# Neighbouring weight columns in a turned projection, and a re-ordered turnover between two MoE layers

## The chip, the cores and the metric

The kernel runs on one core of one Trainium2 chip. The metric is the device time of one execution in microseconds; lower is better. The kernel before was timed in three runs, and one more execution was profiled.

## The reference

Three layers follow each other. Attention over 2 x 8 heads of 768 tokens by 64, in which a query sees only keys with the same six sign bits of a projection. A dense mixture of four experts over the 1536 tokens of width 512: `out += p[:, e] * (relu(x @ w1[e]) @ w2[e])`, hidden width 1024. And a second mixture of eight experts, in which a noisy gate chooses two per token:

```python
noisy_logits = x @ w_gate + log1p(exp(x @ w_noise)) * noise
top2 = argpartition(-noisy_logits, 2)[:, :2]          # weights: softmax of the two
for e in range(8):
    for k in range(2):
        mask = top2[:, k] == e
        out[mask] += top2_w[mask, k, None] * (relu(x[mask] @ w1[e]) @ w2[e])
```

All is float32. The kernel writes each factor of a large matmul as a rounded high part and a rest (`fp32r`, names ending in h and l) and sums three products, so each product of the reference is three matmuls.

## The kernel before, in words

**The second MoE.** The 1536 tokens are routed into a table in DRAM (`tv`), 432 slots (`CAP`) per expert; slots without a token point at padding rows. Expert e needs its rows of `x2d` gathered (GpSimd's indirect DMAs), turned so that the model dimension lies across partitions (`rows`: gh, gl), and its weights loaded and split: a part of 512 KB is loaded into one of four `stage` buffers (`stage_part`, L168, issued by SP), copied to the high part (L175 or L177) and subtracted (L179). For each expert TensorE runs a hidden layer of four parts (`hidden_part`, L212 to L214, 24 matmuls each; relu on ScalarE L217, remainder on VectorE L219) and a projection.

Experts 1 to 6 use the turned projection (`project_turned`, L867 to L869): for each d of four, 24 matmuls with w2 columns as stationary operand and the 432 slots as 432 moving columns. Chunk d takes the columns 4m + d of w2 (`by_chunk`), that is, columns that lie four apart. ScalarE copies the result from PSUM (L871), VectorE transposes it in 32x32 blocks into `yt` (L872), SP stores it to `yd` in DRAM (L876) and loads it back as `ya`, one row per slot (L880). During the next expert `send` multiplies each quarter of `ya` in place by the gate's weight (L691), and GpSimd scatters it into the output with an accumulating indirect DMA (L693). In the same loop VectorE and ScalarE turn the next expert's rows (`turn_blocks`, L855 to L859) and split the next w1 (`load_w1_part`). Experts 0 and 7 use a straight projection (`project`, L233 to L235, 512 moving columns) and multiply and scatter directly (`put`).

**The turnover.** The last expert of the first MoE works in four chunks of tokens. When the last chunk is projected (L716), its three tiles of 128 tokens are stored, turned (`turn_tile`, L563), rated (`tile_logits`, L572), their experts chosen (`choose`, L585 to L601, short operations on 8 columns on VectorE), placed (`place`, L609 to L646: a matmul for the running counts, then two scatters per tile into the table). Expert 0 of the second MoE is split: its first 216 slots (`EARLY`) come from earlier chunks, and its hidden layer (216 moving columns) starts before the last tiles are placed; the three `place` calls stand between its parts. The other 216 slots are fetched after the last scatter (`fetch`: a load of the list `lt` L658, then two gathers L663) and turned (L672 to L676) after three quarters of the early part's second projection. `list_rows` loads the lists of the other experts (L822, L826).

In the last part of the first MoE only TensorE's order is written by hand and a scheduler orders the other engines; from `wt1 = wt1_next` on, the order on every engine and queue is that of the program. w2 of expert 0 is loaded and split inside the first hand-written stretch (`load_w2(w2b, 0, nc.gpsimd)`: both steps on GpSimd). The w1 parts of expert 1 are loaded by SP in order behind `list_rows`. `fetch_blocks` for expert 2 (16 gathers) stands in expert 0's late hidden layer.

## Time and profile before

| | us |
|---|---|
| median of three runs (lowest, highest) | 1178.85 (1178.27, 1178.87) |
| profiled execution, own time | 1177.99 |
| its span | 1176.2 |
| TensorE busy with matmuls | 1145.1 |
| VectorE, GpSimd, ScalarE busy | 607.3, 476.1, 399.8 |
| mean granted TensorE clock, share of full | 0.986 |

The profile is one execution; times in its trace are microseconds from the start of the span. A row of the timeline gives the start, the duration, the engine (PE is TensorE, DVE VectorE, ACT ScalarE, POOL GpSimd, SP SyncE; a q behind the name is its instruction queue, which issues DMAs), the line, the operation, output and inputs, and in brackets a wait ahead of it and who ended it. PEld are weight loads. Matmul durations overlap, so the distance from start to start tells their pace.

### The profile page before, as it was taken

How to read it: one execution, taken by the hardware profiler on the slowest of the kernel's cores; microseconds unless marked ns; L12 is line 12 of the kernel's file. 1: busy time of each engine (PE TensorE's matmuls, PEld its weight loads, DVE VectorE, ACT ScalarE, POOL GpSimd, SP SyncE). 2: the span in 40 equal slices, each digit the busy share in tenths (PEclk: the TensorE clock that was granted, in tenths of full speed). 3: DMA queues.
4: the chain of work that ended last, by engine and by line, in shares of the span. 5: the costliest groups of instructions: out<-in, count | busy, mean ns of one | idle time of the engine just before them, and what ended most of it. 6: DMA issues, size and time to landing. Idle time of an engine off the chain costs nothing. (4 is left out here: it accounts for less than half of the span.)

```text
span 1176.2 us, 16395 instructions
## 1 busy us (share of the span) xinstructions
PE 1145.1 (97%) x6278; PEld 1053.8 (90%) x6279; DVE 607.3 (52%) x1239; ACT 399.8 (34%) x759; POOL 476.1 (40%) x498
## 2 busy tenths in 40 slices
PE   7999999999999999999999999999799999999995
PEld 5999999999899998988999988898689999999993
DVE  7999999985213411242213323356246566656650
ACT  5999998961111100001111111121033333433330
POOL 7888888852001100030001102136377165585233
PEclk9999999999999999999999999997899999999998
DMA  4222222372002200031001200031455556766754
GB/s 137 69 64 66 68 69 68 87 235 72 1 1 65 79 1 1 1 101 43 1 1 54 90 28 28 1 101 41 98 144 165 179 146 195 216 155 200 189 128 58
DMA packets 78539, 101.23 MB, mean 86 GB/s; under 512 B 12944, under 2 KB 54032, under 8 KB 77808
## 3 DMA queue, kind: packets, MB, share of 16 engines
q1 hardware_dynamic: 66888, 84.84, 24.0%
q0 software_dynamic: 9728, 15.18, 6.9%
q8 instruction: 51, 0.84, 0.3%
q10 hardware_dynamic: 1840, 0.11, 0.1%
q14 instruction: 32, 0.26, 0.1%
HBM read 73.30 MB, written 20.90 MB: 80 GB/s over the span
## 5 line engine op out<-in xcount | busy, mean ns | idle before, releaser
L217 ACT ACTIVATE hh<-big 128x768 fp32r<-128x768 f32 (+2 forms) x100 | 81.2, 812 | 495.6 <-PE big L214 467.9
L219 DVE SCALAR_TENSOR_TENSOR hl<-big,hh 128x768 fp32r<-128x768 f32 (+2 forms) x100 | 95.7, 957 | 243.5 <-ACT hh L217 243.2
L233 PE MATMUL sm<-w2h,hh 128*128 128x512 f32 (+1 forms) x448 | 177.5, 397 | 0.0
L234 PE MATMUL sm<-w2l,hh 128*128 128x512 f32 (+1 forms) x448 | 176.3, 394 | 0.0
L212 PE MATMUL big<-xth,w1h 128*128 128x384 f32 x512 | 173.6, 339 | 0.0
L214 PE MATMUL big<-xth,w1l 128*128 128x384 f32 x512 | 172.4, 337 | 0.0
L213 PE MATMUL big<-xtl,w1h 128*128 128x384 f32 x512 | 172.2, 336 | 0.0
L235 PE MATMUL sm<-w2h,hl 128*128 128x512 f32 (+1 forms) x448 | 171.5, 395 | 0.0
L177 POOL TENSOR_SCALAR w1h<-stage 128x1024 fp32r<-128x1024 f32 x18 | 18.8, 1048 | 341.5 <-PE big L213 338.1
L849 POOL DMA_INDIRECT xb<-x2d,at x96 | 112.4, 1171 | 29.4 <-issue 28.7
L251 POOL TENSOR_SCALAR ex<-ex,rec 128x768 f32<-128x768 f32 x96 | 94.0, 979 | 32.6 <-DVE rec L378 21.1
L395 DVE TENSOR_TENSOR el<-sm,eh 128x384 fp32r<-128x384 f32 x192 | 97.5, 547 | 11.8 <-ACT eh L394 10.2
L235 PEld LDWEIGHTS sm<-w2h,hl 128*128 128x128 f32 (+1 forms) x448 | 83.4, 186 | 20.6
L234 PEld LDWEIGHTS sm<-w2l,hh 128*128 128x128 f32 (+1 forms) x448 | 83.7, 187 | 19.5
L212 PE MATMUL big<-gh,w1h 128*128 128x432 f32 (+1 forms) x288 | 101.1, 351 | 0.0
L213 PE MATMUL big<-gl,w1h 128*128 128x432 f32 (+1 forms) x288 | 100.7, 350 | 0.3 <-DVE gl L676 0.3
L214 PE MATMUL big<-gh,w1l 128*128 128x432 f32 (+1 forms) x288 | 100.3, 348 | 0.0
L233 PEld LDWEIGHTS sm<-w2h,hh 128*128 128x128 f32 (+1 forms) x448 | 83.4, 186 | 18.7
L213 PEld LDWEIGHTS big<-xtl,w1h 128*128 128x128 f32 x512 | 96.4, 188 | 1.0
L212 PEld LDWEIGHTS big<-xth,w1h 128*128 128x128 f32 x512 | 96.4, 188 | 0.9
L214 PEld LDWEIGHTS big<-xth,w1l 128*128 128x128 f32 x512 | 96.3, 188 | 0.0
L356 PE MATMUL big<-k,q 128*128 128x512 f32 (+1 forms) x384 | 89.8, 356 | 2.4 <-POOL k L342 2.4
(198 smaller groups left out, 2279.4 us busy)
## 6 DMA issues: line engine op xcount, KB each, us to landing
stage<-in_moe_w_dram SPq DMA_DIRECT2D x96, 512.0 KB
yd<-yt SPq DMA_DIRECT2D x24, 216.0 KB
ya<-yd SPq DMA_DIRECT2D x6, 864.0 KB
out_dram<-zero SPq DMA_DIRECT2D x1, 4096.0 KB
qr<-in_q_dram SPq DMA_DIRECT2D x16, 192.0 KB
kr<-in_k_dram SPq DMA_DIRECT2D x16, 192.0 KB
vr<-in_v_dram SPq DMA_DIRECT2D x16, 192.0 KB
q<-q SPq DMA_DIRECT2D x15, 192.0 KB
```

Of the source, the lines that this page charges most:

```text
L212: nc.tensor.matmul(o, wh[:, d, fs], xh[:, d, cols], start=(d == 0), stop=False)
L213: nc.tensor.matmul(o, wh[:, d, fs], xl[:, d, cols], start=False, stop=False)
L214: nc.tensor.matmul(o, wl[:, d, fs], xh[:, d, cols], start=False, stop=(d == ND - 1))
L217: nc.scalar.activation(hh, pv, AF.Relu)
L219: nc.vector.scalar_tensor_tensor(hl, pv, 0.0, v32(hh), op0=ALU.max, op1=ALU.subtract)
L233: nc.tensor.matmul(o, hh[:, ff, cols], wh[:, ff], start=(f == 0), stop=False)
L234: nc.tensor.matmul(o, hh[:, ff, cols], wl[:, ff], start=False, stop=False)
L235: nc.tensor.matmul(o, hl[:, ff, cols], wh[:, ff], start=False, stop=(f == NF - 1))
L251: engine.tensor_scalar(o, i, scale, bias, op0=ALU.mult, op1=ALU.add)
L356: nc.tensor.matmul(ps[:, n0:n1], w_[:, qs], x_[:, n0:n1], start=st, stop=not st)
L395: nc.vector.tensor_sub(el[:, cs, js], ptv, v32(eh)[:, cs, js])
L849: nc.gpsimd.indirect_dma_start(out=xb[:, b], out_offset=None, in_=x2d.rearrange("t (g x) -> (t g) x", g=4), in_offset=bass.IndirectOffsetO ...
```

## The change

The turned projection takes 128 neighbouring columns of w2 per chunk instead of columns four apart; so `yt` and `yd` hold the columns in another order (g k c instead of k g c, runs of 32), and `send` puts them right while it multiplies, into a new tile with the tag `xg` instead of in place. At the turnover, the last of the four early hidden parts moves behind the hand-over to the full hand-written order; w2 of expert 0 is only loaded in the first stretch, and split by ScalarE and VectorE, two parts ahead of that hidden part and two behind it. `list_rows` is issued by ScalarE instead of SP, and stands behind the turning of the late rows; behind it ScalarE issues the four loads of expert 1's w1, which the splits in expert 0's late projection then use. Of the 16 gathers of `fetch_blocks` for expert 2, four stand behind each late projection of expert 0 and four each in the second and fourth hidden part of expert 1.

```diff
@@ -163,9 +163,9 @@
                             pad_b.rearrange("p j c -> p (j c)").unsqueeze(1).to_broadcast([P, E2, 2 * OVER_J]))
-    def stage_part(src, shape):
+    def stage_part(src, shape, queue=nc.sync):
         st = stage.tile(shape, F32, tag="stage", name="stage")
-        nc.sync.dma_start(st, src)
+        queue.dma_start(st, src)
         return st
     def load_part(wp, bufs, src, shape, tag, engine=nc.gpsimd, rest=nc.vector, staged=None):
@@ -687,8 +687,8 @@
     sent = {}
-    def scatter(y, ps, lt, s, e):
-        nc.vector.tensor_scalar_mul(y, ps, lt[:, s, 1:2].bitcast(F32))
+    def scatter(y, ps, lt, s, e, view=None):
+        nc.vector.tensor_scalar_mul(y if view is None else view, ps, lt[:, s, 1:2].bitcast(F32))
         nc.gpsimd.memset(apart, 0.0)
         ins = nc.gpsimd.indirect_dma_start(out=out, out_offset=bass.IndirectOffsetOnAxis(ap=lt[:, s, 0:1], axis=0),
                                            in_=y, in_offset=None, compute_op=ALU.add)
@@ -777,17 +777,17 @@
         store(t3 + 2, 1)
         chosen = [choose(tile_logits(turned[0]), t3, 1)]
         turned.append(turn_tile(t3 + 1))
-        rows = [ap.tile([P, ND, EARLY], F32R, tag=t, name=t) for t in ("gh", "gl")]
+        first_rows = [ap.tile([P, ND, EARLY], F32R, tag=t, name=t) for t in ("gh", "gl")]
         for s in range(early):
-            turn_rows(rows, s, xgs)
+            turn_rows(first_rows, s, xgs)
         turned.append(turn_tile(t3 + 2))
         chosen.append(choose(tile_logits(turned[1]), t3 + 1, 1))
         parts = []
-        for g in range(NP):
+        for g in range(NP - 1):
             between = (lambda: place(*chosen[2], t3 + 2, 1, base_late)) if g == 2 else None
-            parts.append(hidden_part(g, wt1_next, *rows, EARLY, slice(0, EARLY), between))
+            parts.append(hidden_part(g, wt1_next, *first_rows, EARLY, slice(0, EARLY), between))
             if g == 0:
-                wt2 = load_w2(w2b, 0, nc.gpsimd)
+                staged = [stage_part(w2_part(w2b, 0, r), [P, 2, DM]) for r in range(NP)]
                 chosen.append(choose(tile_logits(turned[2]), t3 + 2, 1))
                 place(*chosen[0], t3, 1, base_late)
             if g == 1:
@@ -819,11 +819,11 @@
     nc.gpsimd.memset(at, 0)
     def list_rows():
-        nc.sync.dma_start(lts[:, 1:].rearrange("p e s c -> p e (s c)"),
+        nc.scalar.dma_start(lts[:, 1:].rearrange("p e s c -> p e (s c)"),
                           tv[1:, 0:CAP].rearrange("e (p s) c -> p e (s c)", p=SLOT_P))
         src = tv[2:, 0:CAP].rearrange("e (b r s) c -> b r e (s c)", b=4, r=BLOCK)
         for b in range(4):
-            nc.sync.dma_start(li[:, 2:, b].rearrange("r e s c -> r e (s c)"), src[b])
+            nc.scalar.dma_start(li[:, 2:, b].rearrange("r e s c -> r e (s c)"), src[b])
     def list_pieces():
         for g in range(4):
@@ -863,13 +863,13 @@
         for f in range(NF):
             g, ff = divmod(f, 2)
             hh, hl = parts[g]
-            wh, wl = (by_chunk(w[:, ff], d) for w in wt[g])
+            wh, wl = (w[:, ff, d * P:(d + 1) * P] for w in wt[g])
             nc.tensor.matmul(ps[:, :CAP], wh, hh[:, ff], start=(f == 0), stop=False)
             nc.tensor.matmul(ps[:, :CAP], wh, hl[:, ff], start=False, stop=False)
             nc.tensor.matmul(ps[:, :CAP], wl, hh[:, ff], start=False, stop=(f == NF - 1))
         yp = padded[d % 2]
         nc.scalar.copy(yp[:, :, :, :BLOCK], ps[:, :CAP].rearrange("p (s b r) -> p s b r", s=SLOT_S, b=4))
-        nc.vector.transpose(yt.rearrange("p s b (c k) -> p k (s b) c", k=ND)[:, d], yp.rearrange("p s b r -> p (s b) r"))
+        nc.vector.transpose(yt.rearrange("p s b (k c) -> p k (s b) c", k=ND)[:, d], yp.rearrange("p s b r -> p (s b) r"))
     def store_turned(yt):
         for g in range(4):
@@ -880,13 +880,18 @@
         nc.sync.dma_start(ya, yd.rearrange("(p s) d -> p s d", s=SLOT_S))
         return ya
     def send(s, ya, e):
-        scatter(ya[:, s], ya[:, s], lts[:, e], s, e)
+        y = mp.tile([SLOT_P, DM], F32, tag="xg", name="xg", bufs=SLOT_S)
+        scatter(y, ya[:, s].rearrange("p (g k c) -> p k g c", g=4, k=ND), lts[:, e], s, e,
+                y.rearrange("p (k g c) -> p k g c", g=4, k=ND))
     with tc.manual_schedule():
         wt1 = wt1_next
+        wt2 = [load_w2_part(w2b, 0, r, engine=nc.scalar, staged=staged[r]) for r in (0, 1)]
+        parts.append(hidden_part(NP - 1, wt1, *first_rows, EARLY, slice(0, EARLY)))
+        wt2 += [load_w2_part(w2b, 0, r, engine=nc.scalar, staged=staged[r]) for r in (2, 3)]
         lt_late, xgs = fetch(mp, SLOT_S, 0, EARLY, early)
-        list_rows()
         rows = new_rows(early)
         give(ap, "xg", early, parts, wt2, lt, 0, 0)
         ps = small()
@@ -894,6 +899,8 @@
         project(ps[:SLOT_P], parts, wt2, mine, 0, 6)
         for s in range(early):
             turn_rows(rows, s, xgs)
+        list_rows()
+        staged = [stage_part(w1_part(w1b, 1, r), [P, ND, FC], nc.scalar) for r in range(NP)]
         project(ps[:SLOT_P], parts, wt2, mine, 6, NF)
         put(ap, "xg", early, ps, lt, 1, 0)
         late = []
@@ -918,8 +925,8 @@
                 if g == 1 and e == 0:
                     list_pieces()
                     xbs[2] = blocks()
-                if g >= 2 and e == 0:
-                    fetch_blocks(2, xbs[2], (g - 2) * 8, (g - 1) * 8)
+                if g in (1, 3) and e == 1:
+                    fetch_blocks(2, xbs[2], 6 + 2 * g, 10 + 2 * g)
             if e + 1 < E2:
                 wt1 = []
                 rows = new_rows(SLOT_S)
@@ -941,8 +948,9 @@
                 for s in range(n):
                     for r in range(s * SLOT_S // n, (s + 1) * SLOT_S // n):
                         turn_rows(rows, r, xgs)
-                        wt1.append(load_w1_part(w1b, e + 1, r, nc.scalar))
+                        wt1.append(load_w1_part(w1b, e + 1, r, nc.scalar, staged[r]))
                     give(mp, "y", 2, parts, wt2, lt_late, s, 0)
+                    fetch_blocks(2, xbs[2], 4 * s, 4 * s + 4)
             else:
                 for s in range(n):
                     give(mp, "xg", SLOT_S, parts, wt2, lts[:, e], s, e)
```

## Rows read from the trace of the kernel before

**Rows 1.** The page, part 1: busy time, share of the span and instructions.
```profile
PE 1145.1 (97%) x6278; PEld 1053.8 (90%) x6279; DVE 607.3 (52%) x1239; ACT 399.8 (34%) x759; POOL 476.1 (40%) x498
```

**Rows 2.** Timeline of TensorE: first matmul of expert 1's hidden layer, projection, and of expert 2.
```profile
872.72 0.36 PE L212 MATMUL big<-gh,w1h 128*128 128x432 f32 x1
...
891.70 0.40 PE L867 MATMUL sm<-hh,w2h 128*128 128x432 f32 x1
...
914.14 0.36 PE L212 MATMUL big<-gh,w1h 128*128 128x432 f32 x1
```

**Rows 3.** Groups by line and shape, weight loads: count, then busy us, mean ns, idle before.
```profile
L867 PEld LDWEIGHTS sm<-hh,w2h 128*128 128x128 f32 x192 | 63.2, 329 | 0.1
...
L212 PEld LDWEIGHTS big<-gh,w1h 128*128 128x128 f32 x288 | 56.8, 197 | 2.4
```

**Rows 4.** Timeline of TensorE at the turnover.
```profile
808.78 0.55 PE L213 MATMUL big<-gl,w1h 128*128 128x216 f32 x1 [0.30 <-DVE gl L676]
...
817.46 0.19 PE L619 MATMUL sm<-both,tri 128*128 128x8 bf16 x1 [1.88 <-DVE both L609]
...
825.48 0.35 PE L212 MATMUL big<-gh,w1h 128*128 128x216 f32 x1
...
828.23 0.40 PE L233 MATMUL sm<-w2h,hh 128*108 128x512 f32 x1
...
844.02 0.97 PE L672 MATMUL sm<-ident,xg 108*128 108x108 f32 x4 [5.97 <-issue]
...
867.07 0.46 PE L233 MATMUL sm<-w2h,hh 128*108 128x512 f32 x1
```

**Rows 5.** Short windows: length, busy PE, PEld, DVE, ACT, POOL, granted clock, DMA share, GB/s.
```profile
808.00:810.00 2.00, 1.70 (x9) 1.48 (x8) 2.00 (x7) 0.58 (x2) 2.00 (x3) 0.62 0.03 8
...
822.00:824.00 2.00, 2.00 (x21) 1.96 (x20) 1.28 (x12) 0.53 (x1) 0.90 (x1) 0.96 0.07 5
...
842.00:844.00 2.00, 0.00 (x0) 0.01 (x1) 0.00 (x0) 0.00 (x0) 0.00 (x0) 0.66 1.10 241
...
848.00:850.00 2.00, 2.00 (x12) 1.77 (x11) 0.75 (x1) 0.00 (x0) 0.11 (x1) 0.64 0.00 0
```

**Rows 6.** Timelines of GpSimd and VectorE at the turnover.
```profile
804.54 2.37 POOL L179 TENSOR_TENSOR w2l<-stage,w2h 128x1024 fp32r<-128x1024 f32 x1
...
804.82 2.11 DVE L585 SCALAR_TENSOR_TENSOR na<-lg 128x8 f32<-128x8 f32 x1
...
819.57 0.16 DVE L585 SCALAR_TENSOR_TENSOR na<-lg 128x8 f32<-128x8 f32 x1
```

**Rows 7.** SP's list and weight loads; landing times of L663, L838 (gathers), L646 (scatters).
```profile
831.40 1.63 SPq L826 DMA_DIRECT2D li<-table  x4
...
833.13 3.15 SPq L168 DMA_DIRECT2D stage<-in_moe_w_dram  x4
...
DMA to landing us min/median/max: 3.7/5.8/8.0
...
DMA to landing us min/median/max: 3.8/3.9/4.0
...
DMA to landing us min/median/max: 2.1/2.5/5.2
```

**Rows 8.** Single lines: splits of w2 and the multiplies, duration in ns min/median/max.
```profile
L175 ACT CAST w2h<-stage x28: 1039/1044/1054, 878.4 to 1137.2; 128x1024 fp32r<-128x1024 f32 x28
...
L179 DVE TENSOR_TENSOR w2l<-stage,w2h x44: 1206/1215/2062, 280.2 to 1138.2; 128x1024 fp32r<-128x1024 f32 x44
...
L691 DVE TENSOR_SCALAR ya<-ya,lts x24: 397/469/534, 946.1 to 1143.6; 108x512 f32<-108x512 f32 x24
...
L691 DVE TENSOR_SCALAR y<-sm,lt x2: 749/750/751, 866.4 to 872.9; 108x512 f32<-108x512 f32 x2
```

**Rows 9.** Timeline in expert 5: the last row tile for expert 6, and its first use.
```profile
1073.60 0.61 DVE L859 TENSOR_TENSOR gl<-tb,gh 128x432 fp32r<-128x432 f32 x1 [0.62 <-ACT gh L858]
...
1079.88 0.36 PE L212 MATMUL big<-gh,w1h 128*128 128x432 f32 x1
```

## The prediction

> **What bounds the kernel now.** The page's first part comes first: TensorE is busy for 1145.1 of 1176.2 us, no other engine for more than 52% [rows 1]. So a change is worth what it takes from TensorE's time, in two ways: matmuls that follow each other faster, or gaps and slow-clock stretches that go. The profiled execution took 1177.99 us, 1.8 us more than its span; the median of the runs is 1178.85, 0.07% above it. I sum against 1177.99; about 0.2% (2.4 us) is what a measurement of this kernel can tell from no change.
>
> The timeline of TensorE's queue comes second, at the borders of one expert of the second MoE. Expert 1's 96 hidden matmuls run from 872.72 to 891.70, its 96 turned-projection matmuls from 891.70 to 914.14 [rows 2]: 197.7 ns against 233.8 ns from start to start, both with 432 moving columns, neither with a gap. The same two durations, 18.99 and 22.44 us, return in the six experts 1 to 6. What differs is the weight load: 197 ns when its 128 columns are neighbours, 329 ns when they lie four floats apart [rows 3]. A hidden part with 216 moving columns shows how fast neighbouring columns can be loaded: 24 loads and matmuls from 825.48 to 828.23, 115 ns each [rows 4]. Twice that is 229 ns, close to the 233.8. I read the turned projection as paced by its weight loads, and the hidden layer with 432 columns as paced by the moving operand.
>
> The same timeline and short windows of the granted clock show the turnover, 808 to 850 us. TensorE waits 0.30, 1.88 and 5.97 us [rows 4]. A window that averages 0.62 between two levels, full (2.4 GHz) and half (1.2 GHz), puts the first fall at 808.5; it rises at 822.2, falls again at 842.6 and rises at 849.4 [rows 5]. The low stretches hold 13.7 and 6.8 us; less the waits in them, TensorE works 11.5 and 5.4 us at half rate, and half of that, 5.75 and 2.7, is lost. Waits and half rate together: 8.15 + 8.45 = 16.6 us. That is all the turnover can give.
>
> **The change, part by part.**
>
> Neighbouring weight columns. Each of 6 x 96 = 576 matmuls then loads a contiguous slice and streams the same 432 columns as the hidden layer, so I take the hidden layer's pace: 22.44 - 18.99 = 3.45 us an expert, **20.7 us** in six. All of it is on TensorE's path. Bounds: 0 if the loads were not the pace; not more than 20.7, as the hidden layer at 432 columns goes no faster in any of seven experts.
> The Trainium skill ("TensorE: Matmul & The Clock Gate", "Part 2: What happens when you issue a matmul") says that weights come through a read port of their own and are pulled ahead of running matmuls; with its "Back-to-back issue gap", N/2.4 + 2.5 ns, 432 columns would take an estimated 182.5 ns whatever the layout, and this part would bring nothing. [rows 2] speak against it: the two stages differ by 36 ns at equal columns. By that rule the sum would be the second rival's.
>
> The permuted output. The projection now leaves VectorE's transposes writing runs of 32 floats instead of single floats 16 bytes apart, at the same count; I take no gain. `send` multiplies out of `ya` through a permuted view into a fresh tile instead of in place. Before, it took 469 ns in the middle; a multiply of 108x512 out of PSUM took 0.75 us [rows 8]. I take 0.75, so +0.28 us on 24 sends, between 0 and, say, a doubling to 0.94. It is covered: in expert 5 the last row tile for the next expert (L859) ends at 1074.21, and TensorE needs it at 1079.88 [rows 9], 5.7 us later. The shorter stage takes 3.45 of these, one longer send ahead of it 0.3; 1.9 us stay, and some of VectorE's present waits are for evacuations that come earlier now. Cost 0. The fresh `ya` reader has a good side: the reload of `ya` no longer waits for the output scatters, so SP is free sooner for the weight loads behind it. Cost and gain 0 on TensorE. In expert 7 the four sends hold all four `xg` buffers until their scatters land, so the first two multiplies of the last expert may wait some microseconds; four PSUM buffers take the four results, and the last multiply does not wait. Cost 0.
>
> w2's split off GpSimd. While GpSimd subtracts (2.37 us), VectorE's 8-element operation takes 2.11 us; the same one takes 0.16 us when GpSimd rests [rows 6]. Five of them are stretched between 804 and 817, and the router's chain behind them is what TensorE waits 1.88 us for (`both`, L609), and probably the 0.30. These waits go. Instead ScalarE copies four parts (1.04 us each) and VectorE subtracts (1.22 each) [rows 8] around the last hidden part. Let t be the end of the third hidden part. Behind relu and remainder of that part the four subtractions end at about t+3.0, 4.2, 6.0 and 7.2, with the fourth part's relu (t+3.5) and remainder (t+4.8) between. TensorE ends the fourth part at t+2.75 and needs a new w2 part every 1.4 us from there, the small half 0.2 us later: t+3.0, 4.4, 5.8, 7.2. I charge **0.3 us**, 0 to 1.5.
>
> The first clock fall. What stands ahead of 808.5 is unchanged, so I let it fall again. The second time the rate rose 5.4 us after work resumed [rows 5]; without the 1.88 us wait I give the first stretch about 4 us of work at half rate, lost **2.0 us** (0 if it does not fall, 5.75 if it stays low as long).
>
> The late gather. Here 5.97 us go. Just ahead of the two gathers SP issues the lists' loads, four of them in 1.63 us, and from 833.13 four 512 KB weight loads in 3.15 us [rows 7]. Gathers took 3.7 to 8.0 us to land here, and 3.8 to 4.0 where no weights were loading [rows 7]. Now these loads and the five list loads stand behind the gathered rows' casts on ScalarE's own queue. The six table scatters follow each other on GpSimd; one lands 2.5 us after its issue in the middle [rows 7], and with the router unhindered the last does so at about t+5. ScalarE reaches the load of the rows' list (`lt`) behind its four copies at t+5.5; with 2.4 us for that load, as small as a scatter, the gathers issue at t+7.9 and t+9.2 and land 3.7 later, t+11.6 and t+12.9. TensorE, through 2.75, 5.6 (867.07 to 872.72, [rows 2, 4]) and three quarters of that again, wants them at t+12.6 and t+13.1. I charge **0.3 us**, 0 to 3; the second clock fall has no cause left.
>
> What the moved loads now meet. ScalarE issues 5 small and 4 large loads, 2.0 + 3.2 us at SP's durations [rows 7], ahead of the relu of expert 0's first late part. TensorE can run two parts (5.5 us) and the rest of a projection (1.4) until it wants that PSUM buffer back; ScalarE's cast, issues and relu and VectorE's remainder end at about 7.6. I charge **0.7**, 0 to 2. The gathers for expert 1 now share the engines with the 2 MB: issued at about 4 us after the casts and landing in up to 8, the first two come 12 to 13.5 us after, and TensorE wants them 12.4 after: **0.5**, 0 to 2; with landings of 4 us the term would be 0.
> The Trainium skill ("DMA: Bandwidth & Descriptors", "Issuing engines are not separate DMA queues") says that the queues of all issuing engines run on the same 16 DMA engines: by that rule the move to ScalarE's queue buys no bandwidth, only another order, and the collision is real (the 0.5); were ScalarE's queue a path of its own, the sum would be 0.5 lower. The loaded landing of 8.0 us, gathers of one queue beside loads of another, agrees with the rule.
> `fetch_blocks` for expert 2 is moved past two scatters; GpSimd has no other work then, and even with the landing at expert 1's projection VectorE starts on them 2 us in. Cost 0.
>
> The sum: turnover 16.6 - (0.3 + 2.0 + 0.3 + 0.7 + 0.5) = 12.8; I take **12.4**, the rest for the small waits I don't see. 1177.99 - 20.7 - 12.4 = 1144.9, forecast **1145 us**. Turnover by the bounds: 16.6 down to 2.35 if every charge came at its upper end; I hold 8 for the likely floor, as the charges are for independent waits. Likeliest case: 1140.7 to 1149.3.
>
> **The rivals.**
> First, the turnover's wait only moves: ScalarE's nine issues and four copies, or the collision, eat most of the 16.6, leaving 2.35 (every charge at its upper end) to 4. For it: ScalarE is one in-order queue and relus stand behind. Against: each is under 1 us by the sums. Time: 1177.99 - 20.7 - 3 = 1154.
> Second, the weight loads are not the pace (other order of operands, PSUM writes), and joining brings nothing: 1177.99 - 12.4 = 1165.6. Against: [rows 3] and the 115 ns of [rows 4].
> Third, slower: VectorE becomes the pace of the six turned stages, because the permuted multiply is far dearer than I take it. From a send of 2.4 us on (0.47 + 1.9) the next expert's rows come late by the rest; to end slower than before it must also cost back 33.1/6 = 5.5 us a stage, that is some 8 us a send. At 10 us: 7.6 late in six stages, less 33.1 gained, 1190. Against: same bytes, runs of 32 floats.
>
> **How the numbers follow.** Forecast 0.82, first rival 0.08, second 0.06, third 0.02; 0.02 for a mixture near no change. The range: from 1140.7 to 1152, which takes in what lies between forecast and first rival; outside stay about 2 in 10. Faster by over 0.2%: 0.82 + 0.08 + 0.06 = 0.96, within 0.02, slower 0.02.
>
> **What would show it.** Six projection stages of 19.0 us with weight loads of about 197 ns; the first wait for `both` gone and VectorE's router operations at 0.15 us throughout; the third hidden part ending about 6 us earlier; no wait over 1 us for the late rows and full clock from 815 on; sends near 0.75 us with no wait of the hidden layer for `gh` or `gl`. The prediction is wrong if the projection keeps 22.4 us, if TensorE waits for ScalarE's relu or w2 between the late gather and expert 1, or if the clock stays at half through the early half of expert 0.

## The result and the profile after

The changed kernel takes 1148.53 us (median of 4 runs, 1146.85 to 1150.78), the kernel before 1178.56 us in the same comparison: a ratio of 0.975 with an interval of 0.973 to 0.977, or 30.0 us less. The forecast was 1145.0 us, the range 1140.7 to 1152.0. The profiled execution is the longest of the four, 1150.78 us with a span of 1149.0, 27.2 us under the profiled execution of before.

The page's first part after, which answers to [rows 1]:

```profile
PE 1120.7 (98%) x6278; PEld 1025.1 (89%) x6279; DVE 595.8 (52%) x1243; ACT 403.1 (35%) x763; POOL 458.7 (40%) x490
```

TensorE's busy time falls by 24.4 us at the same count of instructions: most of the gain is matmuls that take less time, not gaps that went.

TensorE's timeline at the borders of expert 1 (against [rows 2]), then the groups of the turned projection (against [rows 3]; columns: count, busy us, mean ns, idle before):

```profile
867.38 0.36 PE L212 MATMUL big<-gh,w1h 128*128 128x432 f32 x1
...
886.35 0.36 PE L867 MATMUL sm<-hh,w2h 128*128 128x432 f32 x1
...
905.07 0.36 PE L212 MATMUL big<-gh,w1h 128*128 128x432 f32 x1
```

```profile
L867 PEld LDWEIGHTS sm<-hh,w2h 128*128 128x128 f32 x192 | 36.1, 188 | 1.4
...
L867 PE MATMUL sm<-hh,w2h 128*128 128x432 f32 x192 | 68.5, 357 | 0.0
```

The hidden layer keeps its 18.97 us. The turned projection goes from 22.44 to 18.72 us, and its weight load from 329 to 188 ns. The other five turned experts have the same two durations, so the columns give 6 x 3.72 = 22.3 us in this trace.

The turnover in TensorE's timeline (against [rows 4]), with the waits in brackets, and the granted clock in short windows (against [rows 5]; columns as there):

```profile
807.74 0.70 PE L672 MATMUL sm<-ident,xg 108*128 108x108 f32 x4 [0.81 <-DMA xg<-x2d,lt]
809.53 0.70 PE L672 MATMUL sm<-ident,xg 108*128 108x108 f32 x4 [1.09 <-DMA xg<-x2d,lt]
...
836.95 0.70 PE L672 MATMUL sm<-ident,xg 108*128 108x108 f32 x4 [0.33 <-issue]
838.11 0.73 PE L672 MATMUL sm<-ident,xg 108*128 108x108 f32 x4 [0.46 <-DMA xg<-x2d,lt]
...
851.58 0.73 PE L672 MATMUL sm<-ident,xg 108*128 108x108 f32 x4 [0.62 <-DMA xg<-x2d,lts]
853.21 0.73 PE L672 MATMUL sm<-ident,xg 108*128 108x108 f32 x4 [0.91 <-DMA xg<-x2d,lts]
```

```profile
808.00:810.00 2.00, 0.91 (x8) 0.77 (x8) 0.61 (x1) 0.52 (x1) 0.00 (x0) 1.00 0.47 179
810.00:812.00 2.00, 2.00 (x12) 2.00 (x12) 0.68 (x2) 1.21 (x3) 0.00 (x0) 0.54 0.00 0
816.00:818.00 2.00, 2.00 (x16) 2.00 (x15) 0.00 (x0) 0.44 (x1) 0.00 (x0) 0.75 0.00 0
854.00:856.00 2.00, 2.00 (x7) 1.47 (x6) 2.00 (x3) 1.44 (x2) 0.00 (x0) 0.63 0.49 160
```

The waits of 1.88 and 5.97 us are gone. In their place stand three pairs: for the early rows (1.90 us together), the late rows (0.79) and expert 1's rows (1.53). The clock falls after the first pair, to half from 810.2 to 817.0, and after the third, from about 854.5 to 858.0.

An account by stretch makes the profiles comparable. I take the stretch from the first matmul with `both` (L619, near 785 us) to expert 1's first hidden matmul, sum TensorE's waits in it, and sum (1 - granted clock) x length over 1 us windows: that is what half rate costs TensorE if it works all the time. A wait at half rate is counted in both, so the remainder is too small where waits were long.

```
                stretch   waits   half rate   remainder
before           88.76     8.97     10.24       69.55
after            81.61     4.22      5.13       72.26
```

The stretch gives 7.15 us, not the 12.4 of the forecast. The work ahead of it starts 1.8 us later in this execution (785.77 against 783.96; the order there is the same). 22.3 + 7.15 - 1.8 = 27.7 us, and the two profiled executions differ by 27.2: the difference is accounted for.

One more group changed size. VectorE's transposes of the projection's results (L872) and the sends (L691, against the 469 ns of [rows 8]), duration in ns min/median/max; first the transposes in the kernel before, then both after:

```profile
L872 DVE STREAM_TRANSPOSE yt<-padded x24: 1110/1121/1128, 898.3 to 1122.1; 128x512 f32<-128x512 f32 x24
```

```profile
L872 DVE STREAM_TRANSPOSE yt<-padded x24: 704/706/712, 894.6 to 1094.3; 128x512 f32<-128x512 f32 x24
...
L691 DVE TENSOR_SCALAR xg<-ya,lts x24: 444/478/572, 935.4 to 1115.8; 108x512 f32<-108x512 f32 x24
```

The transposes fall by 415 ns, which the forecast had at nothing; the sends stay where they were.

Finally GpSimd's two gathers of the early rows and, just ahead of them, VectorE's two subtractions for parts 0 and 1 of the new `w2`:

```profile
802.81 2.38 DVE L179 TENSOR_TENSOR w2l<-stage,w2h 128x1024 fp32r<-128x1024 f32 x2 [1.31 <-ACT w2h L175]
...
803.01 1.91 POOL L663 DMA_INDIRECT xg<-x2d,lt  x1 [5.54 <-issue]
805.23 1.00 POOL L663 DMA_INDIRECT xg<-x2d,lt  x1 [0.30 <-issue]
```

The forecast had these subtractions around the last hidden part, at 820 to 830 us. They stand behind `wt1 = wt1_next`, from where the order is said to be that of the program, but that did not keep them behind the router's operations, which the program has ahead of them: the scheduler put them at 802 us, where the wait ahead of them, 1.31 us, is for ScalarE's copy. The first gather's issue beside them takes 1.91 us where the second takes 1.00. This is the line that the experiments go after.

### The profile page after: what moved, and what is told of

It is laid out like the page before. It is cut to its first block, busy times and chain, and to the rows that moved or that the text cites. A ratio compares the mean times of both kernels' runs of the same rounds, so it can differ in the third digit from the quotient of the medians.

```text
span 1149.0 us, 16369 instructions
## 1 busy us (share of the span) xinstructions
PE 1120.7 (98%) x6278; PEld 1025.1 (89%) x6279; DVE 595.8 (52%) x1243; ACT 403.1 (35%) x763; POOL 458.7 (40%) x490
## 5 line engine op out<-in xcount | busy, mean ns | idle before, releaser
L219 DVE SCALAR_TENSOR_TENSOR hl<-big,hh 128x768 fp32r<-128x768 f32 (+2 forms) x100 | 95.8, 958 | 246.8 <-ACT hh L217 246.3
L849 POOL DMA_INDIRECT xb<-x2d,at x96 | 104.7, 1091 | 29.3 <-issue 29.3
L235 PEld LDWEIGHTS sm<-w2h,hl 128*128 128x128 f32 (+1 forms) x448 | 83.5, 186 | 20.7
```

The costliest lines, as they stand in the source:

```text
L219: nc.vector.scalar_tensor_tensor(hl, pv, 0.0, v32(hh), op0=ALU.max, op1=ALU.subtract)
L235: nc.tensor.matmul(o, hl[:, ff, cols], wh[:, ff], start=False, stop=(f == NF - 1))
L849: nc.gpsimd.indirect_dma_start(out=xb[:, b], out_offset=None, in_=x2d.rearrange("t (g x) -> (t g) x", g=4), in_offset=bass.IndirectOffsetO ...
```

## The experiments

The runs came in three groups, each on a chip of its own; times are compared within a group, beside the kernel before on that chip (group 1: 1179.55 us; group 2: 1195.09; group 3: 1197.42).

**Group 1: the two halves of the change, apart and together.** First the columns alone: the kernel before with the joined columns, the permuted transposes and the new `send`.

```diff
-            wh, wl = (by_chunk(w[:, ff], d) for w in wt[g])
+            wh, wl = (w[:, ff, d * P:(d + 1) * P] for w in wt[g])
```

> The kernel before with the neighbouring columns alone (the permuted transposes and the permuted send go with them, the turnover is the old one). Theory: the turned projection was paced by its weight loads, and the gain of the columns doesn't depend on the turnover: six projection stages of 18.7 us instead of 22.44, 22.3 us off the kernel before, about 1156.3. Also by it: the second gather for expert 0's early rows is issued about 1.0 us behind the first, since VectorE then runs no split of w2, and TensorE waits about 0.6 us for it. Rival: part of the 22 us comes only with the other turnover (weight loads from DRAM that come late in the shorter stages): then TensorE waits for w1 or w2 and the gain is under 20 us, above 1159.

Measured: 1156.58 us (1155.61 to 1157.27), 23.0 us less, ratio 0.981 (0.979 to 0.982). Loads and transposes are those of after (188 and 704 ns), and the turnover keeps the two old waits, the first of them longer than the 1.88 us of before:

```profile
818.85 0.19 PE L619 MATMUL sm<-both,tri 128*128 128x8 bf16 x1 [5.02 <-DVE both L609]
...
846.31 1.69 PE L672 MATMUL sm<-ident,xg 108*128 108x108 f32 x8 [6.03 <-issue]
```

It follows that the columns carry three quarters of the gain by themselves, with nothing given back.

Then the turnover alone: the kernel after with the old columns, transposes and in-place `send`.

```diff
-            wh, wl = (w[:, ff, d * P:(d + 1) * P] for w in wt[g])
+            wh, wl = (by_chunk(w[:, ff], d) for w in wt[g])
```

> The changed kernel with the old columns (four apart), the old transposes and the in-place send; the turnover is the new one. Theory: the turnover gives what is left of the whole, 30.0 - 22.3 = 7.7 us, about 1170.9, instead of the 12.4 that were forecast, because TensorE still waits for the early gather (about 1.9 us), for expert 1's first two gathers (about 1.5 us) and loses a second stretch at the half clock behind the latter. Rival: the turnover gives the forecast 12.4 (1166.2) by itself and loses in the whole through something that the columns bring.

Measured: 1167.45 us (1163.94 to 1173.99), 12.1 us less, ratio 0.991 (0.987 to 0.994). Here the turnover gives what the forecast said, though the runs reach over 10 us, and its stretch is 76.32 us. In this profile the gather's issue starts 0.09 us ahead of the subtraction, not behind it:

```profile
802.30 1.02 POOL L663 DMA_INDIRECT xg<-x2d,lt  x1 [5.01 <-issue]
803.62 1.00 POOL L663 DMA_INDIRECT xg<-x2d,lt  x1 [0.30 <-issue]
...
802.39 1.23 DVE L179 TENSOR_TENSOR w2l<-stage,w2h 128x1024 fp32r<-128x1024 f32 x1 [1.77 <-ACT w2h L175]
```

Both issues take 1.0 us, TensorE does not wait for the early rows, and the first clock fall is missing. The wait for expert 1's rows is there (1.53 and 0.33 us), with a fall of the clock behind it.

The kernel after again, beside these two:

> The changed kernel again, to have it beside the others on one chip, and a second trace. Theory: the 4 us between its runs (1146.85 to 1150.78) are the first 30 us and the clock: where the mean granted clock is higher, the run is shorter. About 1148.5; in this trace the two waits for expert 1's gathers and for the early gather stand again. Rival: the waits in the turnover were chance of one execution and are absent here.

Measured: 1149.93 us (1142.89 to 1151.91), ratio 0.974 (0.971 to 0.976). The profile shows the slow issue (1.91 us), early waits of 0.58 and 1.02 us, and half clock from 807.9 to 825. The two halves sum to 35.1 us by their medians and the whole gives 29.6; by the ratios they sum to 2.9% and the whole gives 2.7%, which their intervals don't tell apart. That the halves take something from each other is not shown. The runs go largely with the granted clock: 1151.91 us at a mean of 0.984, 1142.89 at 0.994.

Expert 1's gathers earlier: `list_rows` right behind `fetch`, `fetch_rows(1)` ahead of the second early scatter.

```diff
         lt_late, xgs = fetch(mp, SLOT_S, 0, EARLY, early)
+        list_rows()
...
-        list_rows()
+        xgs = fetch_rows(1)
...
-                if g == 0 and e == 0:
-                    xgs = fetch_rows(1)
```

> The changed kernel, with the lists of the other experts loaded right behind the late rows' list, and expert 1's four gathers issued ahead of the second early scatter, so that they are issued before most of w1's 2 MB are in flight; w1's loads stay. Theory: the collision of these gathers with the 2 MB makes TensorE wait 0.6 and 0.9 us and drops its clock for about 3.4 us, so that taking the gathers out of the collision gives back 1.5 + 1.7 = 3.2 us: about 1145.3. Rival: TensorE waits there for something else (ScalarE, busy with issuing nine DMAs, casts late): then the waits stay, and the time is within 1 us of the changed kernel.

Measured: 1146.94 us (1144.90 to 1150.52), ratio 0.974 (0.972 to 0.975). The gathers are issued from 835.0 instead of 846.2 us, and the wait for expert 1's rows (0.31 and 0.66 us in the run of the kernel after beside it, without a fall of the clock of its own) is gone. They land as slowly as before the edit (median 8.8 us, against 8.0). The median is 3.0 us lower than that of the kernel after, but the two sets of runs overlap: the time is not shown to be better.

**Group 2: the race and the collision.** The kernel after was not run on this chip, so no time here says what an edit is worth beside it; the traces say what each edit did. First the subtractions put behind the early rows' second `gl` on VectorE, by an order on that engine alone (`turned_last` is that instruction):

```diff
+        with tc.issue_after(turned_last):
-        wt2 = [load_w2_part(w2b, 0, r, engine=nc.scalar, staged=staged[r]) for r in (0, 1)]
+            wt2 = [load_w2_part(w2b, 0, r, engine=nc.scalar, staged=staged[r]) for r in (0, 1)]
```

> The kernel after, with VectorE's subtractions for the first two w2 parts of the second MoE queued behind its second `gl` of the early rows (same engine, order alone; in the kernel after they stand ahead of the third accumulation of tile 15's group, at 802 us). Theory (a race of 0.2 us at 802 us): in three profiles where such a subtraction had begun before GpSimd issued the first early gather, that issue took 1.91 us, and in the one profile where it had not, 1.02 us; the slow issue puts the second gather 0.9 us later, TensorE waits 1.6 to 1.8 us for the early rows and its granted clock falls. So here: both gather issues 1.0 us, early waits together under 0.6 us, no stretch at the lower clock between 803 and 825 us, 76 to 78 us from the first matmul of `both` to expert 1's hidden part (82.7 in the second profile of the kernel after), time 1143.5 to 1146. Rival (the slow issue comes of something else that stands there, such as the accumulations' traffic or the loads): issue 1.9 us as before, time 1148 to 1151. Third case: the subtractions now delay VectorE's chain of the router by their 2.5 us and the late rows come later: wait for them 2 us or more, time about 1147.

Measured: 1171.03 us (1161.52 to 1172.56), ratio 0.978 (0.974 to 0.981). The trace does most of what the theory says: both issues are fast, there is no half clock anywhere in the stretch, and the stretch is 76.77 us; the early wait is 0.80 us, where under 0.6 was expected.

```profile
802.82 1.02 POOL L663 DMA_INDIRECT xg<-x2d,lt  x1 [5.42 <-issue]
804.15 1.00 POOL L663 DMA_INDIRECT xg<-x2d,lt  x1 [0.30 <-issue]
...
809.95 1.22 DVE L179 TENSOR_TENSOR w2l<-stage,w2h 128x1024 fp32r<-128x1024 f32 x1
811.16 1.22 DVE L179 TENSOR_TENSOR w2l<-stage,w2h 128x1024 fp32r<-128x1024 f32 x1
```

The window from 803 to 860 us (columns as in [rows 5]) has the full clock throughout:

```profile
803.00:860.00 57.00, 52.89 (x360) 46.01 (x359) 28.50 (x110) 17.08 (x34) 20.78 (x24) 1.00 0.39 102
```

The third case came too, in small: the subtractions now stand ahead of the router chain, and TensorE waits 0.98 us for `both`. The absolute time can't be set beside group 1. On this chip TensorE waits another 18.2 us in expert 1's projection, which no profile of group 1 has (last section).

Both edits together:

> The kernel after with two edits at once: the subtractions behind `gl` (as in the run before this) and the lists with expert 1's gathers issued ahead of the second early scatter. If the two causes are separate (the slow first gather; expert 1's rows landing after they are wanted), the gains add: no early wait over 0.3 us, none for expert 1's rows, one short stretch at the lower clock at most, 75 to 76.5 us from `both` to expert 1's hidden part, time 1142 to 1144.5. If the clock's fall is one event that either edit prevents or that comes anyway, it gives what the better of the two gives alone: 1145 to 1147.

Measured: 1167.06 us (1165.88 to 1170.89), ratio 0.976 (0.975 to 0.978), stretch 77.24 us. Expert 1's rows are not waited for, the issues are fast, but the clock falls once, behind the 0.98 us wait for `both`. By this one profile it is the second outcome, that the gains don't add; how far a single profile can be trusted here shows in group 3.

The collision tried from the other side: the four loads of expert 1's `w1` behind the gathers.

```diff
-        staged = [stage_part(w1_part(w1b, 1, r), [P, ND, FC], nc.scalar) for r in range(NP)]
...
+                if g == 1 and e == 0:
+                    staged = [stage_part(w1_part(w1b, 1, r), [P, ND, FC], nc.scalar) for r in range(NP)]
```

> The kernel after with the four loads of expert 1's w1 (2 MB, on ScalarE's queue) issued behind the second relu of the late hidden part instead of ahead of the first: some 5 us later, behind the issues of expert 1's four gathers. Theory (these loads are what the gathers collide with): the gathers land 3.8 to 5 us after their issue instead of 8, TensorE waits under 0.3 us for expert 1's rows (1.0 to 1.5 in the kernel after). Against that, ScalarE's copies of the w1 parts stand between its copies of the rows, and the first part now lands 5 us later, near 853 us, so that a wait for rows may come from there: up to 2 us. Time 1147 to 1150. Rival (the gathers are slow for another reason: their lists' loads, or 108 rows at a time on this queue): landing 7 to 8 us as before and the waits stay; time 1150 to 1153, since the loads too are late.

Measured: 1170.13 us (1167.46 to 1176.64), ratio 0.980 (0.976 to 0.983), stretch 76.78 us. TensorE takes expert 1's rows with no wait:

```profile
850.27 1.14 PE L672 MATMUL sm<-ident,xg 108*128 108x108 f32 x8
```

The early issue is slow here (1.97 us, the subtraction having begun 0.15 us before it), with early waits of 0.38 and 1.09 us. The view of expert 1's gathers has no landing times here, and the vanished wait alone would leave a landing of up to 7.6 us open (issue at 842.68, first use at 850.27). The DMA packets in the trace settle it. Behind the first issue GpSimd's queue moves 192 packets of 4 KB, which hold most of the rows. A quarter of them has ended 3.72 us after that issue and half after 4.62 us, as for the same gathers in the kernel before (3.73 and 4.64), where after has 6.51 and 8.27. The last quarter ends at 11.11 us, as late as in after (11.25), now that the loads run beside it. The collision is shown, for the gathers that TensorE waits for.

**What a weight load pays for distance.** Columns two apart, in the kernel after:

```diff
-            wh, wl = (w[:, ff, d * P:(d + 1) * P] for w in wt[g])
+            wh, wl = (w[:, ff, (d // 2) * 256 + d % 2:(d // 2) * 256 + d % 2 + 255:2] for w in wt[g])
```

> The kernel after with the turned projection's weight columns two apart (0, 2, 4, ... 254 and so on) instead of neighbouring; the output's columns of the six turned experts then come out in another order, with the same work. Before, columns four apart had weight loads of 329 ns and a stage of 22.44 us; neighbouring ones have 188 ns and 18.72 us. If the cost of a load grows evenly with the distance, loads take about 235 ns and the stage, which at 18.72 us is held by the moving columns, stays within 18.7 to 19.5 us: time 1147 to 1155. If any distance other than one costs the whole price: loads 329 ns, stage 22.4 us, time about 1172. If two apart is as good as one: 188 ns, 18.7 us, time as the kernel after.

And eight apart:

```diff
-            wh, wl = (w[:, ff, d * P:(d + 1) * P] for w in wt[g])
+            wh, wl = (w.rearrange("p c d -> p (c d)")[:, 4 * ff + d:4 * ff + d + 1017:8] for w in wt[g])
```

> The kernel after with the turned projection's weight columns eight apart, taken across both 512-column halves of a w2 part; the six turned experts then multiply other columns than the reference's, with the same amount of work. Loads took 188 ns with neighbouring columns, 194 ns with columns two apart and 329 ns with columns four apart. If from there on every column costs a fetch of its own: about 330 ns, stage 22.4 us, 22 us more than the kernel after. If the cost goes on growing with the distance: about 600 ns, and a stage of 40 us or more, over 120 us more.

Measured in the traces: the load (ns, min/median/max) and one projection stage (window, its length, busy times) of the kernel with two apart, then of that with eight apart:

```profile
L867 PEld LDWEIGHTS sm<-hh,w2h x192: 193/194/330, 892.9 to 1119.0; 128*128 128x128 f32 x192
...
949.81:968.62 18.81, 18.81 (x97) 18.68 (x96) 13.73 (x17) 7.21 (x11) 5.73 (x4) 1.00 0.47 132
```

```profile
L867 PEld LDWEIGHTS sm<-hh,w2h x192: 313/344/351, 883.1 to 1140.7; 128*128 128x128 f32 x192
...
948.10:971.62 23.52, 23.52 (x97) 23.51 (x97) 13.94 (x17) 7.50 (x11) 8.11 (x7) 1.00 0.36 104
```

So loads of 188, 194, 329 and 344 ns and stages of 18.72, 18.81, 22.44 and 23.52 us, for columns 1, 2, 4 and 8 floats apart. The price comes whole between two and four apart and hardly grows behind; neither an even growth nor "any distance costs" holds. The times are of one run each. Eight apart takes 1198.75 us, 28.2 more than the kernel after on the same chip (1170.51, group 3), where the six stages give 6 x 4.80 = 28.8. Two apart takes 1176.93 us on the chip of group 2, where the kernel after was not run.

**Group 3: the two edits made better, beside the kernel after.** The subtractions behind the first late tile's `both` (`placed` collects these instructions), and expert 1's loads of `w1` behind the gathers, as above:

```diff
+        with tc.issue_after(placed[-3]):
```

> The kernel after with two edits: VectorE's first two w2 subtractions of the second MoE queued behind the first late tile's `both` (in the run e5_subs_later, behind `gl`, they stood in front of that tile's router chain and TensorE waited 0.98 us for it), and expert 1's w1 loads issued behind the late hidden part's second relu, as in e7_loads_later. If the two causes that were found are separate (the early gather's issue slowed by a VectorE subtraction that began before it; expert 1's gathers landing beside 2 MB of loads): both early issues 1.0 us, no wait for `both` over 0.5 us, none for expert 1's rows over 0.3 us, no lower clock between 803 and 860 us, 74 to 75.5 us from `both` to expert 1's hidden part (82.7 in the kernel after's second profile, 76.8 in each of the two edits alone): 5 to 8 us under the kernel after on the same chip. If the clock falls all the same, 2 to 4 us under it.

> The kernel after once more, on the same chip as the runs beside it, as what they are compared with. By the race: where its profile shows a w2 subtraction begun before the first early gather's issue, that issue takes 1.9 us; where not, 1.0 us, and then the early wait and the fall of the clock at 808 to 825 us are missing too. Ratio to the kernel before 0.972 to 0.977.

> The kernel of e5_subs_later once more, beside the kernel after. Its stretch from `both` to expert 1's hidden part was 76.8 us with no lower clock, against 81.4 and 82.7 us in the two profiles of the kernel after: 4 to 6 us under the kernel after if that was typical, under 2 us if the kernel after often runs without the slow issue.

Measured: the combined kernel 1173.01 us (1164.78 to 1173.77), ratio 0.979 (0.977 to 0.982); the kernel after 1170.51 (1166.71 to 1176.79), 0.980 (0.977 to 0.983); the subtractions behind `gl` 1168.19 (1163.29 to 1173.84), 0.976 (0.973 to 0.979). None is told from another. The combined kernel's trace has no half clock and no wait for `both` or expert 1's rows, but it has a new one, 1.77 us ahead of the late rows' transposes, and its stretch is 76.60 us, not 74 to 75.5. The subtractions behind `gl`, the same kernel as in group 2, now take 82.44 us: waits of 0.88 us for the early rows, 0.98 for `both` and 2.10 for expert 1's rows, and a clock fall behind each. So its 76.77 was not typical. The window that had the full clock in group 2:

```profile
803.00:860.00 57.00, 51.80 (x332) 45.82 (x330) 25.34 (x105) 13.89 (x30) 18.23 (x22) 0.91 0.38 92
```

The stretches of all profiles, in us; "issue" is the first early gather, "early" TensorE's wait for the early rows:

```
                         issue   early   all waits   half rate   stretch
after                     1.91    1.90      4.22        5.13       81.61
after, group 1            1.91    1.60      3.00        8.54       82.92
after, group 3            1.91    2.63      4.65        5.12       81.19
lists first               1.92    1.77      2.71        1.71       76.50
loads later               1.97    1.47      3.03        1.71       76.78
columns two apart         1.92    2.42      5.87       10.24       87.85
columns eight apart       1.90    2.05      4.72        1.71       78.74
turnover alone            1.02    0.00      2.47        1.70       76.32
subs behind gl, group 2   1.02    0.80      4.11        0.00       76.77
subs behind gl, group 3   1.02    0.88      5.21        5.12       82.44
both edits, group 2       1.02    0.90      3.35        1.71       77.24
both edits, group 3       1.02    1.12      4.17        0.00       76.60
```

Stretch less waits less half rate is 71.4 to 72.7 us in every row: these two make the differences, but for 1.3 us. In the upper seven a subtraction had begun before the issue, by 0.15 to 0.22 us; in the lower five it had not. That the order of these two decides 1.9 or 1.0 us, and an early wait of 1.5 us and more or 1.1 and less, is shown. That it decides the time is not: half rate ranges from 1.7 to 10.2 us in the upper rows and from 0 to 5.1 in the lower ones, and the medians of group 3 lie within each other's runs.

## Why the prediction was right, and where it was off

**The columns: 20.7 us forecast, 22.3 in the trace, 23.0 alone on the chip.** The mechanism was right. The bound "not more than 20.7, as the hidden layer at 432 columns goes no faster" was the wrong step: the turned projection now runs at 195.0 ns a matmul (18.72 us / 96), the hidden layer at 197.6. The nearest row was a good estimate and no limit.

**The second rival (the loads are not the pace)** falls by the two runs on distance: with as many columns, the same shapes and the same PSUM writes, the stage follows the load, and the load alone reads w2. With two and eight apart the load engine is busy for 18.68 of 18.81 and 23.51 of 23.52 us. With neighbouring columns it is busy for 18.00 of 18.72, so what holds the 195.0 ns there is open. The 182.5 ns which the forecast worked out from the Trainium skill ("TensorE: Matmul & The Clock Gate", "Back-to-back issue gap"), whose formula is given there for a single isolated matmul, were not reached in any layout.

**The turnover: 12.4 us forecast, 7.15 in the profile of after, 12.1 alone on the chip.** Term by term:

- The `both` wait of 1.88 us and the wait of 5.97 us went, as forecast; VectorE's router operations take under 0.3 us each.
- "What stands ahead of 808.5 is unchanged, so I let it fall again", at 2.0 us: this is the step that failed. The first two w2 subtractions stand at 802 us, not around the last hidden part. The early waits grow from the 0.58 (line below) and 0.30 us of before to 0.81 and 1.09, and half rate lasts for 6.8 us, which costs 3.4: 5.3 us in place of 2.0. The turnover-alone run comes to 76.3 us, where the forecast expected 76.4 (88.76 - 12.4), but that is in part luck: the first fall, charged at 2.0, did not come at all, and expert 1's rows, charged at 0.5, cost 1.9 of waiting and 1.7 of half rate.
- The gathers for expert 1, charged at 0.5 for the collision with the 2 MB of loads: the landing of up to 8 us was right (8.0 to 8.6, against 3.8 to 4.0 in [rows 7]), the size was not. The waits are 1.53 us, and the charge left out that a wait can bring a clock fall: 3.4 us at half rate, 1.7 lost. Here lies the second missing part. "Full clock from 815 on" fell with both.
- The w2 split, 0.3: no wait in this profile; 0.8 to 1.6 us in those of groups 2 and 3. The late gather, 0.3: 0.79 us. ScalarE's issues, 0.7: none; the list and weight loads took it 2.2 and 2.6 us to issue, and TensorE did not wait for the relu.
- The third hidden part was to end 6 us earlier; the fourth begins near 824.0 us (the projection at 826.74 less 2.75), against 825.48 in [rows 4], or 3.3 us earlier counted from `both`.

The charges of 3.8 us so came out at 9.3 (4.22 of waits, 5.1 lost at half rate), which leaves 7.3 of the 16.6. The 16.6 had left out two waits of before, 0.58 us for the early rows and 0.24 for the late ones, so that the sum closes to about 1 us and no better.

```profile
806.17 0.70 PE L672 MATMUL sm<-ident,xg 108*128 108x108 f32 x4 [0.58 <-DMA xg<-x2d,lt]
```

**The VectorE side.** The sends were taken at 750 ns and take 478; the transposes, at "no gain", fall by 415 ns. So the third rival (VectorE paces) is far off. The last row tile for expert 6 still comes in time:

```profile
1051.71 0.61 DVE L859 TENSOR_TENSOR gl<-tb,gh 128x432 fp32r<-128x432 f32 x1 [0.62 <-ACT gh L858]
```

TensorE needs it at 1055.84, 3.5 us later. That the faster transposes bring time is not shown: VectorE is off the path there.

**The first rival (the wait only moves)** came half true. Waits moved to the early rows and to expert 1's rows, and half rate with them, and of 16.6 us 7.15 were gained. The columns gave back 1.6 of the 5.3 us that were missing here; that the two errors had opposite signs is luck, but the time would have stayed inside the range without it. The total of 33.1 us stands against 30.0 measured; the time is off by 3.5 us, as the sum started from 1177.99 and the kernel before took 1178.56 in the comparison.

## What to carry to other kernels

Lay out stationary operands so that neighbouring columns lie next to each other: four floats apart cost 3.7 us per stage of 96 matmuls here, on the engine that set the end, and it needed only another split of the output columns; two floats apart cost next to nothing. When a change takes work from one engine to another, look for where a scheduler will start the new work, not where the code has it: a VectorE subtraction of two SBUF tiles that slid just ahead of a gather's issue cost 0.9 us there, and in all seven such profiles a fall of TensorE's clock followed within 10 us (as it did in one of the five without it). Price a wait on a busy TensorE at its length plus the half rate that may follow, and keep both ends: one and the same program (the subtractions behind `gl`) showed no half rate in one profile and 5.1 us lost to it in another. And take more than one profile before a stretch is called typical.

## What the runs showed of the hardware

**Weight loads and distance.** 188 ns at 1 float apart, 194 at 2, 329 at 4, 344 at 8. The Trainium skill ("SBUF — State Buffer", "Door 1: The DMA port swizzle") says that memory is read in lines of 16 bytes, at full bandwidth with at least two accesses to each line. The trace agrees: two floats apart leave two to a line, four apart one.

**A transpose's writes.** VectorE's transposes of 128x512 floats took 1121 ns with single floats written 16 bytes apart and 706 ns with runs of 32.

**GpSimd's gather beside VectorE.** The first early gather's issue took 1.90 to 1.97 us in seven profiles where a VectorE subtraction of two SBUF tiles (1.2 us) had started just before it, 1.02 us otherwise. The trace of after shows the size of it at other gathers, which take 0.94 us alone: with 0.60 and 1.12 us of a subtraction left at their start they take 1.42 and 1.94, that is, longer by what is left less 0.12 or so. Beside VectorE's L219, whose one input is in PSUM, they take 0.94 to 0.98.

```profile
903.83 1.23 DVE L179 TENSOR_TENSOR w1l<-stage,w1h 128x1024 fp32r<-128x1024 f32 x1
904.46 1.42 POOL L849 DMA_INDIRECT xb<-x2d,at  x1 [0.30 <-issue]
...
910.93 1.06 DVE L219 SCALAR_TENSOR_TENSOR hl<-big,hh 128x864 fp32r<-128x864 f32 x1 [2.88 <-ACT hh L217]
911.66 0.94 POOL L849 DMA_INDIRECT xb<-x2d,at  x1 [0.30 <-issue]
...
916.65 1.22 DVE L179 TENSOR_TENSOR w2l<-stage,w2h 128x1024 fp32r<-128x1024 f32 x1
916.74 1.94 POOL L849 DMA_INDIRECT xb<-x2d,at  x1 [0.30 <-issue]
```

The Trainium skill ("SBUF — State Buffer", "SBUF: two separate sides") has a port pair that the two engines share, taken whole by the one that starts first while "the other fully blocks". The trace agrees where VectorE starts first. Where a gather's issue starts first it does not: with the gather 0.09 us ahead the subtraction took 1.23 us, as it does alone.

**A long wait on two chips.** In the eight profiles of groups 2 and 3, the two on distance among them, TensorE waits 12 to 21 us in sum between 862 and 925 us; in the profiles of group 1 and of after there is no such wait. In the subtractions-behind-`gl` run of group 2, TensorE's and ScalarE's lines are these:

```profile
881.24 0.36 PE L214 MATMUL big<-gh,w1l 128*128 128x432 f32 x1
...
906.25 0.73 PE L867 MATMUL sm<-hh,w2h 128*128 128x432 f32 x1 [18.24 <-ACT hh L217]
...
905.30 0.89 ACT L217 ACTIVATE hh<-big 128x864 fp32r<-128x864 f32 x1 [23.65 <-remote]
```

The relu waits for the last matmul of the hidden part. The trace has this matmul at 881.24 us, but the semaphore that it raises, and that ScalarE waits on, goes up at 905.28 us, so the view finds nobody who ended the wait. GpSimd issues 28 gathers one behind the other meanwhile, 866.6 to 902.5 us; these alone don't make the wait, as in the profile of after GpSimd issues its gathers as densely, 871.5 to 921.2 us, and no engine waits like this. The kernel before is 15.5 and 17.9 us longer on these chips too, so it probably has this wait, but it was not profiled there. Why the signal comes late stays open, and so does whether gathers spread over more time would shorten the wait.
